# Moving transposes of x, wk, q and k from the PE to the DMA crossbar in a tuned attention and token-MLP kernel

## The chip, the cores and the metric

The kernel runs on one core of one Trainium2 chip. The metric is the device time of one execution in microseconds (us). In a ratio, the mean time of one kernel's fast runs is divided by the mean of the other's fast runs of the same rounds, so it is not quite the ratio of the medians quoted beside it. A run is called slow if it lies over 1.5% above the fastest of its kernel. A single run has no known state.

Names: PE is the matmul engine, PEld its weight loads, DVE the vector engine, ACT the scalar engine, POOL the GpSimd engine, SP or SyncE the engine that issues most DMAs. SBUF is the on-chip memory of the tiles, PSUM the one that PE's results go to. A DMA *lands* when its data have arrived.

## The reference, cut to what matters

```
def _attn_ref(q, k, v):                      # 8 batches, 12 heads, 448 positions, 64 wide
    scores = scale * np.matmul(q, k.transpose(0, 1, 3, 2)) - np.log(S)
    attn = 1.0 / (1.0 + np.exp(-scores))     # a sigmoid, no row sums
    return np.matmul(attn, v)
def _moe_ref(x, w_q, w_k, w_out):            # x: the heads side by side, 448 x 768
    wq, wk = x @ w_q, x @ w_k                # 768 -> 64
    W_tok = scale * np.einsum('bsd,btd->bst', wq, wk)
    mixed = np.einsum('bst,btd->bsd', W_tok, x)
    return np.maximum(mixed, 0.0) @ w_out
```

## The kernel before

Two batches and two heads form a pair. There are 24 pairs, in four units of six. A unit is two batches; its six pairs make the whole x of those batches, and then its MLP can run. The kernel's matmuls contract over the partitions, so q, k, x and wk are needed in a second, transposed layout. The kernel before makes all of these on the PE, with an identity matrix, into PSUM, and DVE copies the result out.

The order of work is written by hand. A string of letters says what is emitted next: S is one scores block and its sigmoid, P one block of values, q or k a transposition for a later pair, x the transposition of a finished piece of x, W a step of x times the weights, N the transposition of wk, U and M (or m) the mixing and its relu, O a block of the output.

```
def tr(n, nm, split=False):                        # letters q and k
    fb, ps = bank([P, NI, 2, NP], BF16, "pt" + nm)
    t16 = ld.pop((nm + "16", n))
    for i in range(NI):                            # seven 128x128 transposes
        nc.tensor.transpose(ps[:, i]..., t16[:, i]..., ident16)
    t = p_qk.tile([P, 2, NI, NP], BF16, tag=nm + "t", name=nm + "t")
    ...                                            # DVE copies ps to t
```

Inputs are float32. A load (448 KB, issued by SyncE) brings a pair's q, k or v; GpSimd casts it to bf16; the transposition reads the cast. The helper `pump` keeps both going. The cast of q or k needs one of two bf16 buffers, and a load needs a float32 buffer that an earlier cast has emptied:

```
def pump_loads():
    ...
            if n >= 3 and (nm, n - 3) not in cast:
                break
            load1(n, nm, nc.sync)                  # SyncE, in the order of emission
def pump():
    ...
            back = 3 if nm == "v" else 2           # v has three buffers, q and k two each
            if n >= back and (nm, n - back) not in used:
                break
            cast1(n, nm, nc.gpsimd)                # GpSimd, in the order of emission
        cast.add((nm, n))
        pump_loads()
...
        elif t in "qk":
            tr(c, t)
            used.add((t, c))
            pump()                                 # at once: next cast, next load
```

So right after each q or k transposition, the cast that reuses its buffer is emitted, and right after this the load that reuses the cast's float32 buffer. Loads, casts and stores stand in this order in their engines' queues.

## Time and profile before

| | before |
|---|---|
| median | 210.54 us (210.08 to 210.99, 2 runs) |
| span in the profile | 209.4 us |
| PE busy | 197.0 us, 94% |
| ACT busy | 170.8 us, of which the 168 sigmoids 155.4 |
| sigmoids | from 6.47 to 177.70 us |

A page row of slices shows, for 40 equal parts of the span, the busy share in tenths. A row of groups shows the source line, the engine, the operation with its tiles, the number of instructions, then busy us and the mean in ns, then the idle time before them and what ended it. The lines of the kernel before are in the prediction.

### The profile page before, as it was taken

The page shows a single profiled execution, that of the slowest core. Times are in us where ns is not written, and L with a number is a line of the kernel's source. Part 1 is how long each engine was busy: PE and PEld are TensorE (multiplying, and loading weights), DVE is VectorE, ACT ScalarE, POOL GpSimd, SP SyncE. Part 2 cuts the span into 40 slices and gives each one's busy share as a digit, 9 for nine tenths or more (in the row PEclk, how much of TensorE's full clock was granted, in tenths as well). Part 3 has the DMA queues.
Part 4 walks back from the last instruction along what each step waited for, and adds up shares of the span by engine and source line. Part 5 has one row for each costly group of instructions (what it writes and reads, how often), then busy time and mean ns, then how long its engine had stood idle before and what let it go on. Part 6 is the DMA issues. An engine that isn't in the chain of part 4 may idle for free.

```text
span 209.4 us, 6320 instructions
## 1 busy us (share of the span) xinstructions
PE 197.0 (94%) x2630; PEld 117.5 (56%) x2630; DVE 121.9 (58%) x208; ACT 170.8 (82%) x193; POOL 72.6 (35%) x85
## 2 busy tenths in 40 slices
PE   8498988889999999999999999999999999999991
PEld 7254544556546656656656565655565555655561
DVE  2135555755598746664889675645788654554321
ACT  3689999979999999999998989889898998055220
POOL 2477755577877842730022700251110000000000
PEclk9759999999999999999999999999999999999999
DMA  5999999999999999997065463355203252154785
GB/s 174 374 381 380 381 173 290 381 384 384 383 384 383 379 381 385 399 389 253 5 199 130 145 181 79 78 147 195 51 29 78 75 152 70 27 134 104 200 203 174
DMA packets 28684, 47.59 MB, mean 227 GB/s; under 512 B 5360, under 2 KB 24432, under 8 KB 28656
## 3 DMA queue, kind: packets, MB, share of 16 engines
q1 hardware_dynamic: 27616, 45.03, 67.1%
q10 hardware_dynamic: 1040, 2.16, 2.7%
q8 instruction: 20, 0.33, 0.7%
q14 instruction: 8, 0.07, 0.1%
HBM read 36.18 MB, written 11.01 MB: 225 GB/s over the span
## 4 chain that ended last, share of the span: by engine, by line
PE 75%; DMA 16%; POOL 2%; SPq 1%; ACT 1%; issue 1%; DVE 1%; DVEq 0%; ACTq 0%; POOLq 0%
PE po L283 27%; PE sc L154 15%; PE pv L173 13%; DMA v<-in_v_dram 9%; DMA k<-in_k_dram 8%; PE px L191 5%; PE pw L215 3%; PE ptq L131 3%; PE ptk L131 3%; PE pt L240 3%; PE pm L264 2%; ACT at L159 1%; POOL k L118 1%; POOL v L118 1%; SPq L107 1%; PE pk L227 1%
## 5 line engine op out<-in xcount | busy, mean ns | idle before, releaser
L159 ACT ACTIVATE at<-sc,bias_t 128x896 bf16<-128x896 f32 x168 | 155.4, 1020 | 12.6 <-PE sc L154 11.7
L283 PE MATMUL po<-wout,mx 128*128 128x384 bf16 (+1 forms) x342 | 60.6, 324 | 0.0
L154 PE MATMUL sc<-qt,kt 64*64 64x448 bf16 x672 | 57.7, 367 | 2.5 <-ACT at L159 1.8
L283 PEld LDWEIGHTS <-mx 128*128 128x128 bf16 x342 | 30.9, 98 | 24.3 <-issue 7.0
L173 PE MATMUL pv<-at,v 64*64 64x448 bf16 x672 | 41.8, 352 | 1.1 <-POOL v L118 1.1
L178 DVE CAST xt<-pv 128x896 bf16<-128x896 f32 x24 | 26.2, 1091 | 23.4 <-PE pv L173 23.4
L308 DVE COPY o<-po 128x384 f32<-128x384 f32 x45 | 25.1, 557 | 24.7 <-PE po L283 24.4
L154 PEld LDWEIGHTS <-kt 64*64 64x64 bf16 x672 | 21.9, 105 | 23.7 <-issue 12.6
L118 POOL CAST q<-q 128x896 bf16<-128x896 f32 x23 | 21.5, 933 | 33.3 <-issue 26.3
L118 POOL CAST v<-v 128x896 bf16<-128x896 f32 x24 | 22.3, 934 | 22.6 <-PE pv L173 18.0
L118 POOL CAST k<-k 128x896 bf16<-128x896 f32 x23 | 21.5, 933 | 19.4 <-PE ptk L131 15.7
L173 PEld LDWEIGHTS <-v 64*64 64x64 bf16 x672 | 20.5, 107 | 11.2 <-POOL v L118 1.4
L138 DVE COPY kt<-ptk 128x896 bf16<-128x896 bf16 x23 | 14.3, 620 | 10.3 <-PE ptk L131 10.2
L196 DVE COPY xn<-px 128x512 bf16<-128x512 bf16 x48 | 18.0, 417 | 2.9 <-PE px L191 2.9
L306 ACT COPY o<-po 128x384 f32<-128x384 f32 x10 | 4.8, 478 | 15.7 <-PE po L283 15.7
L256 DVE TENSOR_SCALAR mx<-pm 128x896 bf16<-128x896 f32 x15 | 16.3, 1088 | 1.8 <-PE pm L264 1.4
L138 DVE COPY qt<-ptq 128x896 bf16<-128x896 bf16 x23 | 14.1, 619 | 4.5 <-PE ptq L131 3.7
L131 PE MATMUL ptq<-ident,q 128*128 128x128 bf16 x161 | 13.7, 228 | 1.4 <-POOL q L118 1.4
L191 PE MATMUL px<-ident,xt 128*128 128x128 bf16 x192 | 14.7, 220 | 0.2 <-DVE o L308 0.2
L191 PEld LDWEIGHTS <-xt 128*128 128x128 bf16 x192 | 11.6, 98 | 4.6 <-issue 3.8
L131 PE MATMUL ptk<-ident,k 128*128 128x128 bf16 x161 | 13.3, 224 | 0.6 <-POOL k L118 0.6
L131 PEld LDWEIGHTS <-q 128*128 128x128 bf16 x161 | 9.9, 102 | 6.7 <-issue 3.7
(43 smaller groups left out, 93.8 us busy)
## 6 DMA issues: line engine op xcount, KB each, us to landing
q<-in_q_dram SPq DMA_DIRECT2D x24, 448.0 KB, 8.0
v<-in_v_dram SPq DMA_DIRECT2D x24, 448.0 KB, 7.5
k<-in_k_dram SPq DMA_DIRECT2D x23, 448.0 KB, 7.8
out_dram<-o SPq DMA_DIRECT2D x44, 192.0 KB, 3.0
w<-in_moe_w_out_dram SPq DMA_DIRECT2D x6, 384.0 KB, 5.8
out_dram<-o ACTq DMA_DIRECT2D x10, 192.0 KB, 3.2
wqk<-in_moe_w_q_dram SPq DMA_DIRECT2D x2, 192.0 KB, 9.4
wqk<-in_moe_w_k_dram SPq DMA_DIRECT2D x2, 192.0 KB, 8.5
```

The lines of the kernel that those rows point to most:

```text
L118: eng.tensor_copy(out=t16.rearrange("p i b d -> p b i d"), in_=ld.pop((nm, n)).rearrange("p b (i d) -> p b i d", i=NI),)
L131: nc.tensor.transpose(ps[:, i].rearrange("p h n -> p (h n)"), t16[:, i].rearrange("p b d -> p (b d)"), ident16,)
L138: nc.vector.tensor_copy(out=t[:, hs], in_=ps[:, :, hs, :].rearrange("p i h n -> p h i n"))
L154: nc.tensor.matmul(sc[HALF[h], b2, 0:S], qk["k", n][HALF[b2], h, i, :], qk["q", n][HALF[b2], h].rearrange("p i n -> p (i n)"), start=True, ...
L159: nc.scalar.activation(at, sc[:, :, 0:S], ACTF.Sigmoid, bias=bias_t, scale=attn_scale)
L173: nc.tensor.matmul(ps[HALF[b2], h, 0:S], ld["v16", n][HALF[h], i, b2, :], ats[n, i][HALF[h], b2, :], start=(i == 0), stop=(i == NI - 1),)
L178: nc.vector.tensor_copy(out=xts[j][:, :, 0:S], in_=ps[:, :, 0:S])
L191: nc.tensor.transpose(ps[:, m, h].rearrange("p b d -> p (b d)"), xts[j][:, h, m * P : (m + 1) * P], ident16,)
L196: nc.vector.tensor_copy(out=xns[u][:, :, b2, 2 * HD * j : 2 * HD * (j + 1)].rearrange("p m (h d) -> p m h d", h=2), in_=ps[:, :, :, b2, :],)
L256: nc.vector.tensor_scalar(dst, ps, moe_scale, 0.0, ALU.mult, ALU.max)
L283: nc.tensor.matmul(ps, mxs[u][c].rearrange("p b s -> p (b s)")[:, m * P : (m + 1) * P], wout16[:, c, w0:w1], start=(c == 0), stop=(c == NC ...
L308: nc.vector.tensor_copy(out=o[:, nb * NB : (nb + 1) * NB], in_=ps)
```

## The change

The intent is to relieve the PE: from pair 12 on, q and k go through the crossbar of the DMA engines, SBUF to SBUF (letters a and b, 24 transfers of 229 KB), and so do x (X, 12 of 262 KB) and wk (n, 2 of 262 KB) of the two middle units. The layouts change to what the crossbar gives, q and k get 14 buffers instead of 8 so as to be transposed early, the weight load is halved, the start is reordered, and the string of letters is planned anew with the output blocks moved to where the PE is freed.

```
-    p_qk = pool("qk", 8)
+    p_qk = pool("qk", 14)
...
+    def tr_dma(n, nm):
+        t16 = ld.pop((nm + "16", n))
+        t = p_qk.tile([P, NI, P], BF16, tag=nm + "t", name=nm + "t")
+        nc.sync.dma_start_transpose(out=t, in_=t16.rearrange("p i b d -> p (i b d)"))
+        qk[nm, n] = t
...
+    def tr_x_dma(n):
+        u, j = pairs[n]
+        nc.sync.dma_start_transpose(
+            out=xn_of(u, j).rearrange("p h m x -> p (h m) x"),
+            in_=xts[j].rearrange("p h s -> p (h s)"),
+        )
...
+        if dma:        # in mlp_wkn
+            nc.sync.dma_start_transpose(
+                out=wkn[u].rearrange("p b m x -> p (b m) x"), in_=wqk.rearrange("p b s -> p (b s)")
+            )
+            return
...
+    def cast_weights():
+        nc.gpsimd.tensor_copy(out=wqk16[HALF[0]], in_=wqk32)
+        nc.gpsimd.dma_start(out=wqk16[HALF[1]], in_=wqk16[HALF[0]])
...
-        "SPPPSkqSWWWSWWWWSWWWWSWSx",
-        "SNPSPPPPSPPSUSqSMUmSMq",
...
+        "SPPPPSkSkWSWWWSWWWWSWWWWSbx",
+        "SSPPPPNSPPPSUSaSMaSb",
+        "SSMUXSbSMSaSPPPSPPPPX",
+        "SamaSMSbmPPPPSPPPXSOSS",
...
-        elif t in "qk":
-            tr(c, t)
-            used.add((t, c))
+        elif kind in "qk":
+            (tr if t == kind else tr_dma)(c, kind)
+            used.add((kind, c))
             pump()
```

More of the change, by code (lines that the diff above doesn't have):

```diff
@@ L84 @@
     wqk16 = singles.tile([P, H, P], BF16, name="wqk16")
-    wqk32 = singles.tile([P, H, P], F32, name="wqk32")
+    wqk32 = singles.tile([NP, H, P], F32, name="wqk32")
     ident = singles.tile([P, P], F32)
@@ L125, with tr @@
     qk = {}
-    def tr(n, nm, split=False):
-        fb, ps = bank([P, NI, 2, NP], BF16, "pt" + nm)
+    def tr(n, nm):
+        fb, ps = bank([P, NI, P], BF16, "pt" + nm)
         t16 = ld.pop((nm + "16", n))
         for i in range(NI):
-            nc.tensor.transpose(
-                ps[:, i].rearrange("p h n -> p (h n)"),
-                t16[:, i].rearrange("p b d -> p (b d)"), ident16,
-            )
-        t = p_qk.tile([P, 2, NI, NP], BF16, tag=nm + "t", name=nm + "t")
-        def evac(hs):
-            nc.vector.tensor_copy(
-                out=t[:, hs], in_=ps[:, :, hs, :].rearrange("p i h n -> p h i n")
-            )
+            nc.tensor.transpose(ps[:, i], t16[:, i].rearrange("p b d -> p (b d)"), ident16)
+        t = p_qk.tile([P, NI, P], BF16, tag=nm + "t", name=nm + "t")
+        nc.vector.tensor_copy(out=t, in_=ps)
         qk[nm, n] = t
         free1.append(fb)
-        if split:
-            return evac
-        evac(slice(0, 2))
+    def tr_dma(n, nm):
+        t16 = ld.pop((nm + "16", n))
+        t = p_qk.tile([P, NI, P], BF16, tag=nm + "t", name=nm + "t")
+        nc.sync.dma_start_transpose(out=t, in_=t16.rearrange("p i b d -> p (i b d)"))
+        qk[nm, n] = t
     ats = {}
@@ L154, in scores @@
                 nc.tensor.matmul(
-                    sc[HALF[h], b2, 0:S], qk["k", n][HALF[b2], h, i, :],
-                    qk["q", n][HALF[b2], h].rearrange("p i n -> p (i n)"), start=True, stop=True,
+                    sc[HALF[h], b2, 0:S].rearrange("p (i n) -> p i n", i=NI),
+                    qk["k", n][HALF[b2], i, HALF[h]], qk["q", n][HALF[b2], :, HALF[h]],
+                    start=True, stop=True,
                 )
@@ L182, with xn_of @@
     xns = {}
+    def xn_of(u, j):
+        if j == 0:
+            xns[u] = p_x.tile([P, NJ, 2, 4, P], BF16, tag="xn", name="xn")
+        return xns[u][:, j]
     def tr_x(n):
         u, j = pairs[n]
-        if j == 0:
-            xns[u] = p_x.tile([P, 4, 2, D], BF16, tag="xn", name="xn")
-        fb, ps = bank([P, 4, 2, 2, HD], BF16, "px")
+        fb, ps = bank([P, 2, 4, P], BF16, "px")
         for h in range(2):
             for m in range(4):
-                nc.tensor.transpose(
-                    ps[:, m, h].rearrange("p b d -> p (b d)"), xts[j][:, h, m * P : (m + 1) * P],
-                    ident16,
-                )
-        for b2 in range(2):
-            nc.vector.tensor_copy(
-                out=xns[u][:, :, b2, 2 * HD * j : 2 * HD * (j + 1)].rearrange(
-                    "p m (h d) -> p m h d", h=2
-                ),
-                in_=ps[:, :, :, b2, :],
-            )
-        free1.append(fb)
+                nc.tensor.transpose(ps[:, h, m], xts[j][:, h, m * P : (m + 1) * P], ident16)
+        nc.vector.tensor_copy(out=xn_of(u, j), in_=ps)
+        free1.append(fb)
+    def tr_x_dma(n):
[4 more added lines that the diff above has]
+        )
     wkn, tmps, mxs = {}, {}, {}
@@ L215, in mlp_wqk @@
                 nc.tensor.matmul(
-                    ps[HALF[x], b2, 0:S], wqk16[HALF[b2], h, 64 * x : 64 * x + 64],
+                    ps[HALF[x ^ b2], b2, 0:S], wqk16[HALF[b2], h, 64 * x : 64 * x + 64],
                     xts[h // 2][HALF[b2], h % 2, 0:S], start=(h == 0), stop=(h == H - 1),
@@ L221, in mlp_wqk, with mlp_wkn @@
             free2.append(fb)
-    def mlp_wkn(u):
-        fb, ps = bank([P, 4, 2, P], BF16, "pk")
+    def mlp_wkn(u, dma=False):
+        wkn[u] = p_one.tile([P, 2, 4, P], BF16, tag="wkn", name="wkn")
+        if dma:
[3 more added lines that the diff above has]
+            return
+        fb, ps = bank([P, 2, 4, P], BF16, "pk")
         for b2 in range(2):
             for m in range(4):
-                nc.tensor.transpose(ps[:, m, b2, :], wqk[:, b2, m * P : (m + 1) * P], ident16)
-        wkn[u] = p_one.tile([P, 4, P], BF16, tag="wkn", name="wkn")
-        nc.vector.tensor_copy(
-            out=wkn[u], in_=ps.rearrange("p m b x -> p m (b x)")[:, :, 64:192]
-        )
+                nc.tensor.transpose(ps[:, b2, m], wqk[:, b2, m * P : (m + 1) * P], ident16)
+        nc.vector.tensor_copy(out=wkn[u], in_=ps)
         free1.append(fb)
@@ L240, in mlp_tmp @@
                 nc.tensor.matmul(
-                    ps[HALF[b2]], wkn[u][:, m, 64 * b2 : 64 * b2 + 64],
-                    xns[u][:, m, b2, nb * NB : (nb + 1) * NB],
+                    ps[HALF[b2]].rearrange("p (x d) -> p x d", d=HD), wkn[u][:, b2, m, HALF[1 - b2]],
+                    xns[u].rearrange("p j h m x -> p (j h) m x")[:, 6 * nb : 6 * nb + 6, m, HALF[b2]],
                     start=(m == 0), stop=(m == 3),
@@ L326, in load_weights @@
     def load_weights():
-        for b2 in range(2):
-            for x, w in enumerate((moe_w_q, moe_w_k)):
-                o = 64 * (x ^ b2)
-                nc.sync.dma_start(
-                    out=wqk32[HALF[b2], :, o : o + 64], in_=w.rearrange("(h d) n -> d h n", d=HD)
-                )
+        for x, w in enumerate((moe_w_q, moe_w_k)):
+            nc.sync.dma_start(
+                out=wqk32[:, :, 64 * x : 64 * x + 64], in_=w.rearrange("(h d) n -> d h n", d=HD)
+            )
+    def cast_weights():
+        nc.gpsimd.tensor_copy(out=wqk16[HALF[0]], in_=wqk32)
+        nc.gpsimd.dma_start(out=wqk16[HALF[1]], in_=wqk16[HALF[0]])
     def load_wout(c):
@@ L336, in load_wout @@
         nc.sync.dma_start(out=w32[c], in_=moe_w_out[c * P : (c + 1) * P, :])
+    PLAN = (
+        "SSSKSSSkqPPPPS",
+        "SPkSqSSPqSPqSkSPP",
+        "SPPPSxPSPSSPPSkSkP",
+        "SPPPPSSqSkSqqSPPPSx",
+        "SqPSSPPPSqSSxSxq",
+        "SPPPPSPPPSkSqSSxkPPSPk",
+        "SPPPPSkSkWSWWWSWWWWSWWWWSbx",
+        "SSPPPPNSPPPSUSaSMaSb",
+        "SSMUXSbSMSaSPPPSPPPPX",
+        "SamaSMSbmPPPPSPPPXSOSS",
+        "SbOaSPPPPSPPPXSOSSSO",
+        "SaSPPPSPPPPXSOSSSOO",
+        "SPPPSPPPPXSbSWWWWWSWWWWSWWWSa",
+        "SPPPSPPPPSnaSSSUUXSbO",
+        "SMSbSPPPPSPPPXSOSMSO",
+        "SMOSMSbOSMSOaSSMOPPPP",
+        "SPPPXSbSPPSPPPPPXSOSS",
+        "SbOSPPPPSPPPXSOSSSaO",
+        "SPPPPSPPPXSaSWWSWWWWWSWWWWWSO",
+        "SSSnOSPPPSPPPPSUUS",
+        "SMOOSSPPPPPPPSOSMSbOSM",
+        "SxOSPPPSPPPPSOSMSOxSM",
+        "SxOmPPSPPPPPSOSSSOOS",
+        "SOxSPPPSPPPPSOSSWWWWxS",
+        "WWWPPPPWPPPWWOxWWOONOUUMMMOOOmMmOOOOOOOOOOOOOOOO",
+    )
     IA, IB = slice(0, 4), slice(4, 7)
@@ L349, in cols @@
         return slice(r.start * HD, r.stop * HD)
-    nc.sync.dma_start(out=q0, in_=src["q"])
-    nc.sync.dma_start(out=k0[:, :, cols(KA)], in_=src["k"][:, :, cols(KA)])
-    nc.sync.dma_start(out=k0[:, :, cols(KB)], in_=src["k"][:, :, cols(KB)])
+    for t32, nm in ((q0, "q"), (k0, "k")):
+        for b2, eng in ((0, nc.sync), (1, nc.scalar)):
+            eng.dma_start(out=t32[:, b2], in_=src[nm][:, b2])
     nc.vector.memset(zeros, 0.0)
@@ L362, with keep_warm @@
     nc.scalar.activation(warm, bias_t, ACTF.Sigmoid, bias=bias_t, scale=1.0)
-    fb, ps = bank2("pwarm")
-    for _ in range(32):
-        nc.tensor.matmul(ps[:, 0, 0:P], zeros, zeros, start=True, stop=True)
-    free2.append(fb)
+    def keep_warm(n):
+        fb, ps = bank([P, 512], F32, "pwarm")
+        for _ in range(n):
+            nc.tensor.matmul(ps[:, 0:P], zeros, zeros, start=True, stop=True)
+        free1.append(fb)
+    keep_warm(32)
     for t in xts + [wqk]:
         nc.vector.memset(t[:, :, S:], 0.0)
-    ORDER = [("q", 1), ("k", 1), ("v", 0)]
-    nq = 2
-    for n in range(1, N):
-        for _ in range(2 if n in (1, 2, 3, 4) else 1):
-            if nq < N:
-                ORDER += [("q", nq), ("k", nq)]
-                nq += 1
-        ORDER.append(("v", n))
-    for n, at_ in ((0, 18), (1, 30), (2, 33), (3, 36), (4, 39), (5, 42), (6, 45)):
-        ORDER.insert(at_, ("w", n))
+    STEPS = "".join(PLAN)
+    ORDER, seen = [], dict(q=1, k=1, P=0)
+    first = {}
+    for t in STEPS:
+        t = dict(a="q", b="k").get(t, t)
+        if t in "qkP":
+            if t != "P":
+                ORDER.append((t, seen[t]))
+            elif seen[t] % NI == 0:
+                ORDER.append(("v", seen[t] // NI))
+            seen[t] += 1
+        first.setdefault(t, len(ORDER))
+    places = [(first["W"] - 9, 0)] + [(first["O"] - 14 + 2 * c, c) for c in range(1, 7)]
+    for n, (place, c) in enumerate(places):
+        ORDER.insert(place + n, ("w", c))
+    CASTS = list(ORDER)
+    n = CASTS.index(("w", 0))
+    CASTS.insert(n + 3, CASTS.pop(n))
     used, loaded, cast = set(), set(), set()
@@ L396, in pump @@
     def pump():
-        while len(cast) < len(ORDER) + 2:
-            nm, n = ORDER[len(cast) - 2]
+        while len(cast) < len(CASTS) + 2:
+            nm, n = CASTS[len(cast) - 2]
             if (nm, n) not in loaded:
@@ L405, in pump @@
                 else:
-                    nc.gpsimd.tensor_copy(out=wqk16, in_=wqk32)
+                    cast_weights()
             else:
@@ L425 @@
     for nm in "qk":
-        qk[nm, 0] = p_qk.tile([P, 2, NI, NP], BF16, tag=nm + "t", name=nm + "t")
+        qk[nm, 0] = p_qk.tile([P, NI, P], BF16, tag=nm + "t", name=nm + "t")
     def tr_part(nm, t16, r, e, b=None):
-        shape = [P, r.stop - r.start, 2, NP]
+        shape = [P, r.stop - r.start, P]
         fb, ps = (None, ps_q.tile(shape, BF16, tag=b, name="pt" + nm)) if b else bank(shape, BF16, "pt" + nm)
@@ L432, in tr_part @@
             nc.tensor.transpose(
-                ps[:, i - r.start].rearrange("p h n -> p (h n)"),
-                t16[:, i].rearrange("p b d -> p (b d)"), ident16,
+                ps[:, i - r.start], t16[:, i].rearrange("p b d -> p (b d)"), ident16,
             )
-        COPY[e](out=qk[nm, 0][:, :, r], in_=ps.rearrange("p i h n -> p h i n"))
+        COPY[e](out=qk[nm, 0][:, r], in_=ps)
         if fb:
@@ L441 @@
     tr_part("q", q016, IB, "s")
+    keep_warm(5)
     tr_part("k", k016, KA, "v", free2[-1])
+    keep_warm(3)
     used |= {("q", 0), ("k", 0)}
     pump()
-    PLAN = (
-        "SSSKqSSSSkq",
-        "SPPPPPSkSSPkSPqSS",
-        "SxPqSPPPPSPPSqSPPSkPSPP",
-        "SxPSSPkSSSkPPSkP",
-        "SPPPPSqSqSSqxSxSk",
-        "SSqkPPSPPPPSPqSkSSxPPPP",
-        "SPPPSkqSWWWSWWWWSWWWWSWSx",
-        "SNPSPPPPSPPSUSqSMUmSMq",
-        "SkSMxSkSPPPSPPPPSqSk",
-        "SMxmqSPPPPSPPPSOSSSOO",
-        "SSkxSSOkSPPPSPPPPSO",
-        "SSSqOkSPPPSPPPPSqxSPPPP",
-        "SPPPSOSSSqOxSWWWWWSWW",
-        "SWWWWWSOSSSNxPPPPPSPPSUU",
-        "SMSxkSPPPPSPPPSOSMSkO",
-        "SMmOkSMSOqSMSqOSPPPPSPPP",
-        "SOSSSkOxSPPPSPPPPSxO",
-        "SSSOOSSxOSPPSPPPPPPPPP",
-        "SPPPSxqSWSWWWWWWSWWWSWWOS",
-        "SSONSSOxSPPPPPPSPSUU",
-        "SSMxOSSPPPPPPPSOSMSkx",
-        "SPPPSPPPPmOSMmqOSMSOqSS",
-        "SkOxSPPPPSPPPSOSSSOOx",
-        "SPSPPPPPPSOSSSOOxS",
-        "WPPPWPPPPWWWWWWWWWWOONxOUUMmmOOmMmOOOOOOOOOOOOOOOO",
-    )
-    done = dict.fromkeys("SPqkKxWNUMO", 0)
+    done = dict.fromkeys("SPqkKxWNUMOD", 0)
     done["q"] = done["k"] = 1
-    for t in "".join(PLAN).replace(" ", ""):
-        kind = "M" if t == "m" else t
+    for t in STEPS:
+        kind = dict(m="M", a="q", b="k", X="x", n="N").get(t, t)
         c = done[kind]
@@ L492 @@
                 pump()
-        elif t in "qk":
-            tr(c, t)
-            used.add((t, c))
+        elif kind in "qk":
+            (tr if t == kind else tr_dma)(c, kind)
+            used.add((kind, c))
             pump()
+        elif t == "D":
+            fb, ps = bank([P, 512], F32, "pwarm")
+            for x in range(2):
+                nc.tensor.matmul(
+                    ps[HALF[x], 0:S].rearrange("p (i n) -> p i n", i=NI), zeros[HALF[0], 0:64], qk["q", 0][HALF[0], :, HALF[x]],
+                    start=True, stop=True,
+                )
+            free1.append(fb)
         elif t == "K":
@@ L500 @@
             tr_x(c)
+        elif t == "X":
+            tr_x_dma(c)
         elif t == "W":
             mlp_wqk(*divmod(c, H))
-        elif t == "N":
-            mlp_wkn(c)
+        elif kind == "N":
+            mlp_wkn(c, t == "n")
         elif t == "U":
```

## The prediction

> **What bounds the kernel now.** I read the page first: busy shares, then the slices.
>
> ```profile
> PE 197.0 (94%) x2630; PEld 117.5 (56%) x2630; DVE 121.9 (58%) x208; ACT 170.8 (82%) x193; POOL 72.6 (35%) x85
> ...
> PEclk9759999999999999999999999999999999999999
> DMA  5999999999999999997065463355203252154785
> ...
> L159 ACT ACTIVATE at<-sc,bias_t 128x896 bf16<-128x896 f32 x168 | 155.4, 1020 | 12.6 <-PE sc L154 11.7
> ```
>
> PE is busy almost all the time, but ACT is close behind, and a mean share hides that the two take turns. The clock is full except at the start. The DMA engines are full up to slice 18 (about 95 us) and a third to a half busy afterwards. The sigmoid row is the second limit: 168 sigmoids cost 155.4 us whatever PE does, and ACT waited only 12.6 us for PE before them. Next come busy times by stage:
>
> ```profile
> 60.00:100.00 40.00, 39.96 (x588) 24.40 (x590) 26.69 (x45) 38.91 (x44) 20.03 (x22) 1.00 0.99 363
> 100.00:140.00 40.00, 40.00 (x565) 23.50 (x558) 27.68 (x43) 35.93 (x39) 11.58 (x13) 1.00 0.43 118
> 140.00:177.00 37.00, 37.00 (x494) 21.80 (x496) 24.98 (x42) 33.78 (x38) 2.80 (x3) 1.00 0.34 94
> 177.00:209.40 32.40, 27.91 (x256) 16.60 (x248) 11.92 (x20) 9.70 (x17) 0.00 (x0) 1.00 0.55 144
> ```
>
> The columns are stretch, length, then PE, PEld, DVE, ACT, POOL busy, clock, DMA share, GB/s. From 60 us to 177 us PE is never idle, while ACT idles 1.1, 4.1 and 3.2 us. So the middle is PE-bound, by a narrow margin. After 177 us there are no sigmoids; this tail is PE alone. The ACT timeline shows the margin as small gaps before scores:
>
> ```profile
> 103.02 6.65 ACT L159 ACTIVATE at<-sc,bias_t 128x896 bf16<-128x896 f32 x7 [0.48 <-PE sc L154]
> 109.95 1.01 ACT L159 ACTIVATE at<-sc,bias_t 128x896 bf16<-128x896 f32 x1 [0.28 <-PE sc L154]
> ```
>
> It also gives three fixed points: the first sigmoid starts at 6.47, the last (176.69, 1.01 long) ends at 177.70, and 29 in a row take 26.25 us, so one costs 0.905 us. A PE timeline gives what PE pays for each kind of work, by start-to-start times (the second column includes pipeline drain):
>
> ```profile
> 160.51 0.55 PE L131 MATMUL ptq<-ident,q 128*128 128x128 bf16 x7
> 161.00 0.76 PE L154 MATMUL sc<-qt,kt 64*64 64x448 bf16 x12
> 161.69 0.56 PE L131 MATMUL ptk<-ident,k 128*128 128x128 bf16 x7
> 162.09 1.14 PE L283 MATMUL po<-wout,mx 128*128 128x384 bf16 x6
> 163.07 0.61 PE L191 MATMUL px<-ident,xt 128*128 128x128 bf16 x8
> 163.61 0.38 PE L154 MATMUL sc<-qt,kt 64*64 64x448 bf16 x4
> 163.82 0.93 PE L173 MATMUL pv<-at,v 64*64 64x448 bf16 x16
> ```
>
> Seven transposes of q or k cost 0.49 before 64-wide work (161.00 - 160.51) and 0.40 before full-array work; eight of x 0.54. A group of four scores or values costs about 0.19 to 0.23, a block of six output matmuls 0.98. Changing between 64*64 and 128*128 work costs about 0.1.
>
> **What the Trainium skill says.** "VectorE: DVE Perf Modes", section "The three transpose paths", gives 390 ns for a 128x128 transpose on TensorE and 1309 ns on the DMA crossbar. The trace has 220 to 228 ns per PE transpose and, pipelined, 0.40/7 = 57 ns; no DMA transpose has run yet. "DMA: Bandwidth & Descriptors", section "Latency and other measured facts", gives a DMA transpose 261 GB/s, or 350 to 400 when contiguous. The trace before has only plain transfers, but warns about small pieces: the wqk weight rows (256 B each) pull a full DMA from 380 down to about 130 GB/s, in this view of 20 to 30 us in 40 slices:
>
> ```profile
> GB/s 380 387 373 373 387 387 380 373 380 380 380 387 380 373 387 387 366 387 387 380 380 387 373 387 387 422 303 309 257 193 134 133 134 119 126 129 131 142 115 142
> ```
>
> The same page, section "Anatomy of one DMA — SWDGE (gpsimd) path", says that DMA engines do not wait on semaphores; the wait happens on the issuing sequencer before dispatch. The trace agrees: SyncE's queue itself waits, and everything behind waits too.
>
> ```profile
> SPq L318 <- DVE o L308: 48.4, 20, 7.2
> SPq L107 <- POOL k L118: 14.7, 8, 10.7
> ```
>
> **The change part by part.**
>
> *Removed from PE:* 24 q/k sets of 7 transposes, 12 x sets of 8, 2 wk sets of 8: 24 x 0.45 + 12 x 0.54 + 2 x 0.54 = 18.4 us, all on the bounding engine before 177 us. DVE loses their evacuations (24 x 0.62, 24 half copies of 0.42, two of wk), but it was not the limit.
>
> *Why not 18 us faster:* ACT takes over as bound. I added up each row of both plans (seven sigmoids a row) with the PE costs above and, for ACT, 0.905 per sigmoid and 0.8 per relu. Before, rows 9 to 23 sum to PE 107.3 against ACT 98.2; the trace takes 108.3 (68.4 to 176.7), so the bookkeeping holds. Summing the larger of PE and ACT over all 24 rows gives 165.2 before, against 171.2 measured (6.47 to 177.70): 3.4 of the remaining 6 us are start gaps (1.77, 0.16, 0.25, 1.25), 2.6 spread out. After, ACT alone sums to 154.4 (two relus fewer). PE is far below it in rows 7 to 14 and above it only in rows 15 and 20 to 23, by 1.3 + 1.4 + 1.1 + 0.7 + 0.5 = 5.1, because output blocks moved there. So 159.5, plus 1 us of start gaps and 2 spread out: 162.5.
>
> *Start:* the first k needs all 448 KB instead of 192, so the first sigmoid slips from 6.47 to about 7. In return three scores follow at once after the second k part, which should close the 1.77 gap; the two duplicate weight loads (256 B rows, issues of 2.74 and 3.75 us on SyncE) are replaced by an on-chip copy. Both are in the 1 us above.
>
> *Tail:* from 176.4, PE works until 205.1, 28.7 us. The new last row has 4 wqk steps fewer (-0.76), 2 output blocks more (+1.96): about 30.0.
>
> *Sum without new waits:* sigmoids end at 7 + 162.5 = 169.5; the tail starts 1.3 before, 168.2, and ends at 198.2; final stores 4.3 (205.1 to 209.4 now): 202.5 span; the unprofiled time is 1.1 above the span: 203.6 us.
>
> *Added:* 38 DMA transposes, 24 x 229 KB + 14 x 262 KB = 9.2 MB, all on SyncE's queue. At the 261 GB/s of the page that is 35 us of DMA (estimate), at the 130 of the 256 B pieces 70 us. They fall between about 55 and 140 us. Half of that has a full DMA now, but q and k transposes have a lead of 15 to 48 sigmoids (14 to 43 us) over their first use, thanks to 14 buffers instead of 8. The x ones lead by about 10 us, wk by about 6 us after its last matmul. I add 0.9 us for waits: **204.5 us**.
>
> **Rivals.**
>
> *ACT bounds earlier than hoped, or gains vanish in local bunching.* Rows 15 and 20 to 23 stay PE-bound and only three PSUM pairs buffer scores. Against: my sums already charge this. If the spread-out idle doubles: 206 to 207, "same".
>
> *SyncE's queue becomes the limit.* In the changed order a load often follows a transpose, and waits for a GpSimd cast that needs the buffer which that transpose reads. Thus one load holds up the queue for a transpose's whole latency plus 0.93 of cast. Ahead of the first wk transpose there is such a chain: x, k, load, load, load, q, wk. If a transpose takes 2 to 3 us, wk lands about when tmp needs it; at 6 us PE waits several us, twice, and stores back up behind. That makes 207 to 215.
>
> *The DMA rate becomes the limit.* Loads, stores and weights needed by 140 us are about 42 MB, 110 us at 380 GB/s. With 35 us of transposes this just fits; with 70 it lags by 40, more than the leads: 215 or more. For it: 256 B pieces at 130 GB/s. Against: those read HBM, these read SBUF.
>
> *The transposes are hidden but PE cools.* In rows 7 to 9 PE is only 55 to 70% busy; between 5 and 10 us a 46% busy PE lost its clock (0.81, then 0.50). Gaps here are under 1 us, so I hold it unlikely.
>
> **Range and chances.** With no waits and a better start, 201; with a few us of waiting for wk or x, 208 to 211. Range 200.5 to 211. Faster by over 2% means below 206.3: 0.62. Within 2%: 0.23. Slower, if queue or rate limits: 0.15.
>
> **What would show it.** Right: PE busy down by about 18 us to 179; ACT above 95% from 60 to 168 us; last sigmoid ending near 169.5; tail of 30 us; no long waits of PE weight loads for DMA transposes. Wrong: PE waiting for xn, wkn, kt or qt from DMA; SyncE waiting long for GpSimd casts; DMA at 9 in slices 18 to 27 with GB/s well below 380; PEclk below 9 in the middle; a transpose taking over 5 us from issue to landing.

## The result and the profile after

The changed kernel takes **295.4 us** (294.8 to 296.01, 2 runs) against 210.54: ratio 1.4031, 95% interval 1.3852 to 1.4211. Its outputs are correct. The prediction, 204.5 us and most likely faster, is wrong by 91 us.

From the page of the changed kernel: the busy row, the slices, and two groups.

```profile
PE 200.7 (68%) x2358; PEld 107.1 (36%) x2358; DVE 103.1 (35%) x149; ACT 168.7 (57%) x190; POOL 72.4 (25%) x86
...
PE   8788989850340846843800689968804999999993
...
ACT  3999999980060348560830188859900688941421
...
PEclk9999999975555689795865599979975899999998
DMA  7999989996667758789297536949998234404686
...
L156 ACT ACTIVATE at<-sc,bias_t 128x896 bf16<-128x896 f32 x168 | 156.1, 1021 | 96.3 <-PE sc L150 95.6
```

Up to slice 8 (59 us) PE and ACT are about as busy as in the kernel of before. From then on PE and ACT both stop and start again, and the granted clock falls to half in the stops. ACT now waits 95.6 us for scores, where it waited 11.7. The DMA engines are not the obvious limit: there are slices with 2 to 5 tenths among them. What holds up the PE shows in the list of waits (engine, line, what it waits for; us in total, times, longest), all engines of the changed kernel:

```profile
POOL k L118 <- DMA kt<-k: 48.1, 6, 15.4
POOL q L118 <- DMA qt<-q: 41.6, 5, 11.4
...
PE pv L170 <- POOL v L118: 35.8, 6, 14.2
...
PE pt L241 <- DMA wkn<-wqk: 29.5, 2, 17.3
```

PE hardly waits for a transposed q or k, which I had looked at, with its lead of 14 to 43 us. It waits for the **cast of v**, which no part of the change touches (35.8 us), and for wk, in two stops (29.5 us). The transposes of wk are late before they begin: they are issued at 158.97 and 221.40 us and land 5.4 and 3.2 us later, but by the time of the issue PE has stood for 11.8 and 8.9 us. GpSimd in its turn waits 89.7 us for crossbar transposes to leave the bf16 buffers. The timelines of 57 to 80 us show how these hang together. SyncE's queue of the changed kernel (start, us, engine, line, transfer):

```profile
57.60 2.39 SPq L140 DMA_TRANSPOSE kt<-k  x1
67.52 0.36 SPq L339 DMA_DIRECT2D w<-in_moe_w_out_dram  x1
67.93 0.43 SPq L107 DMA_DIRECT2D k<-in_k_dram  x1
68.41 0.46 SPq L107 DMA_DIRECT2D v<-in_v_dram  x1
68.91 0.47 SPq L107 DMA_DIRECT2D k<-in_k_dram  x1
69.42 1.40 SPq L140 DMA_TRANSPOSE qt<-q  x1
77.50 0.37 SPq L107 DMA_DIRECT2D q<-in_q_dram  x1
77.91 0.47 SPq L107 DMA_DIRECT2D v<-in_v_dram  x1
```

GpSimd of the changed kernel, same stretch (in brackets the idle time before it, and what ended it):

```profile
65.79 0.93 POOL L118 CAST k<-k 128x896 bf16<-128x896 f32 x1 [8.17 <-DMA kt<-k]
66.67 0.83 POOL L452 CAST wout<-w 128x768 bf16<-128x768 f32 x1
76.54 0.93 POOL L118 CAST q<-q 128x896 bf16<-128x896 f32 x1 [9.04 <-DMA qt<-q]
77.41 0.93 POOL L118 CAST v<-v 128x896 bf16<-128x896 f32 x1
```

Follow it once. At 57.60 SyncE issues a transposition of k. The next cast of k needs the buffer that it reads, so it starts only at 65.79, 8 us later. The cast of wout stands behind it on GpSimd and ends at 67.50. The load that needs the buffer of that cast is the next entry of SyncE's queue, so SyncE stands from 60.0 to 67.5. Only then come the loads behind it, and the next transposition at 69.42. Then it goes round again: 76.54, 77.50. The cast of v at 77.41 stands behind the cast of q, and PE needs that v. ACT's timeline shows the price:

```profile
61.82 3.70 ACT L156 ACTIVATE at<-sc,bias_t 128x896 bf16<-128x896 f32 x4 [0.55 <-PE sc L150]
80.22 1.01 ACT L156 ACTIVATE at<-sc,bias_t 128x896 bf16<-128x896 f32 x1 [14.70 <-PE sc L150]
```

The DMA view of the same 57 to 80 us in 40 slices says that the engines stand still in ten of the slices while PE waits, so their rate alone does not hold up this stretch. In most of the others they are full, so the landings of 7 to 8 us contain their rate too:

```profile
DMA  9999999999982800000097999899999370000938
```

I call this **the loop**: transposition, cast into its buffer, load into that cast's buffer, next transposition. The 24 q and k transposes are issued from 57.6 to 233.5 us, one per 7.6 us on the mean (175.9/23), while their own issue takes 1.2 to 3.3 us.

### The profile page after: what moved, and what is told of

The parts are those of the page before. It is cut to its first block, busy times and chain, and to the rows that moved or that the text cites. A ratio compares the mean times of both kernels' runs of the same rounds, so it can differ in the third digit from the quotient of the medians.

```text
span 294.2 us, 5749 instructions
## 1 busy us (share of the span) xinstructions
PE 200.7 (68%) x2358; PEld 107.1 (36%) x2358; DVE 103.1 (35%) x149; ACT 168.7 (57%) x190; POOL 72.4 (25%) x86
## 4 chain that ended last, share of the span: by engine, by line
PE 29%; DMA 11%; issue 8%; SPq 8%; ACT 2%; DVE 2%; POOL 2%; DVEq 0%; ACTq 0%; POOLq 0%
PE po L284 15%; PE sc L150 4%; PE pv L170 4%; DMA out_dram<-o 3%; DMA kt<-k 3%; SPq L140 3%; DMA wkn<-wqk 3%; PE pt L241 2%; SPq L197 2%; ACT at L156 2%; DMA qt<-q 2%; PE pw L213 2%; SPq L319 2%; SPq L107 1%; DVE xt L175 1%
## 5 line engine op out<-in xcount | busy, mean ns | idle before, releaser
L156 ACT ACTIVATE at<-sc,bias_t 128x896 bf16<-128x896 f32 x168 | 156.1, 1021 | 96.3 <-PE sc L150 95.6
L170 PE MATMUL pv<-at,v 64*64 64x448 bf16 x672 | 48.2, 396 | 37.1 <-POOL v L118 35.8
L150 PE MATMUL sc<-qt,kt 64*64 64x448 bf16 x672 | 62.4, 384 | 9.9 <-ACT at L156 7.3
L241 PE MATMUL pt<-xn,wkn 128*64 128x384 bf16 x64 | 9.3, 448 | 29.5 <-DMA wkn<-wqk 29.5
L257 DVE TENSOR_SCALAR mx<-pm 128x896 bf16<-128x896 f32 x19 | 20.5, 1090 | 5.5 <-PE pm L265 5.5
L213 PE MATMUL pw<-xt,wqk 64*64 64x448 bf16 x192 | 13.8, 398 | 9.1 <-DVE xt L175 9.1
L241 PEld LDWEIGHTS <-wkn 128*64 128x64 bf16 x64 | 4.3, 142 | 33.2 <-DMA wkn<-wqk 30.1
L213 PEld LDWEIGHTS <-wqk 64*64 64x64 bf16 x192 | 7.0, 121 | 13.0 <-issue 9.6
L192 DVE COPY xn<-px 128x1024 bf16<-128x1024 bf16 x12 | 8.3, 688 | 5.8 <-PE px L191 5.8
L265 PE MATMUL pm<-wqk,tmp 64*64 64x448 bf16 x96 | 9.2, 401 | 0.7 <-ACT at L156 0.6
L133 DVE COPY kt<-ptk 128x896 bf16<-128x896 bf16 x11 | 6.8, 620 | 7.6 <-PE ptk L131 7.6
```

The source lines that it names most:

```text
L150: nc.tensor.matmul(sc[HALF[h], b2, 0:S].rearrange("p (i n) -> p i n", i=NI), qk["k", n][HALF[b2], i, HALF[h]], qk["q", n][HALF[b2], :, HAL ...
L156: nc.scalar.activation(at, sc[:, :, 0:S], ACTF.Sigmoid, bias=bias_t, scale=attn_scale)
L170: nc.tensor.matmul(ps[HALF[b2], h, 0:S], ld["v16", n][HALF[h], i, b2, :], ats[n, i][HALF[h], b2, :], start=(i == 0), stop=(i == NI - 1),)
L213: nc.tensor.matmul(ps[HALF[x ^ b2], b2, 0:S], wqk16[HALF[b2], h, 64 * x : 64 * x + 64], xts[h // 2][HALF[b2], h % 2, 0:S], start=(h == 0), ...
L241: nc.tensor.matmul(ps[HALF[b2]].rearrange("p (x d) -> p x d", d=HD), wkn[u][:, b2, m, HALF[1 - b2]], xns[u].rearrange("p j h m x -> p (j h ...
L257: nc.vector.tensor_scalar(dst, ps, moe_scale, 0.0, ALU.mult, ALU.max)
```

## The experiments

The theory is the loop. The rivals: the crossbar's **rate** (too many bytes in small pieces), the **new plan** itself (a bad order even without DMA transposes), and the **rest of the change** (layouts, start, weights). All kernels of one group ran on one chip, beside runs of the kernel before of 209.7 to 210.7 us median (one run, 212.2 us, beside the kernel that costs the transposition). All but the four marked "wrong" gave correct outputs. "One run" means that the state is unknown.

### Which part: all on PE, four buffers, each part alone

Every a, b, X and n of the plan goes back to q, k, x and N; nothing else changes:

```
-        "SSMUXSbSMSaSPPPSPPPPX",
+        "SSMUxSkSMSqSPPPSPPPPx",
```

> The changed kernel with every crossbar transpose put back on the PE (new plan, layouts, buffers and start kept). Both theories, that of the loop through the shared in-order queues and that of a slow crossbar, say the loss comes from the DMA transposes alone: 206 to 213 us. If the new plan or the new tile layouts are at fault, over 230 us.

Measured: 228.39 us, ratio 1.0845 (1.0785 to 1.0905). Without the DMA transposes 67 of the 295 us are gone, so most of the loss is theirs. But the new plan on the PE costs 18 us more than the old, which I had not expected. In its waits of the PE stands `px<-xt` with 12.0 us in 10 times: in the new plan x follows right behind the values whose copy by DVE it needs. With x by the crossbar (the second of the two runs of parts below) PE does not have this wait.

Two more bf16 buffers for each of q and k:

```
-    p_c16 = pool("c16", 2)
+    p_c16 = pool("c16", 4)
-                back = 3 if nm == "v" else 2
+                back = 3 if nm == "v" else 4
```

(and 12 instead of 14 buffers of q and k, for room).

> Four buffers instead of two for the cast q and k, casts running up to four ahead (12 instead of 14 buffers for the transposed tiles, for space). Theory 'loop': a cast waits for the transpose that reads its buffer, the v cast and the next load wait behind that cast, and the next transpose waits behind that load; with two more buffers the loop opens and the time falls below 240 us, GpSimd's waits for kt and qt from 90 us to under 20. Rival 'crossbar rate': 38 transposes at some 4.5 us each are the limit whatever the buffers, time stays over 280 us.

Measured: 260.01 us, ratio 1.2358 (1.2284 to 1.2432). It helps by 35 us, not by the most of it, and neither expectation came. GpSimd still waits 45.7 us for transposes (90 before) and PE 22.1 for v. With more buffers `pump` runs ahead as far as they allow, and then again the next cast is the one that needs the buffer just given to the crossbar.

The changed kernel with only q and k by DMA, and with only x and wk:

> Only q and k from pair 12 on by DMA; x and wk on the PE. Theory 'loop': most of the loss stays, 260 to 290 us. If the loss comes from PE's waits for wk and x, it falls below 230 us.

> Only x and wk of the two middle units by DMA; q and k on the PE. Theory 'loop': no cast waits for a transpose, so 205 to 218 us, with PE waits of a few us for wk. Rival 'crossbar rate': 14 of 38 transposes, so some 14/38 of the 85 us, 235 to 245 us.

Measured, one run each: 265.71 and 222.81 us. With q and k alone PE waits 26.4 us for v and 19.2 for xt. With x and wk alone it waits 6.5 for xt and 2.7 for wk, and the time lies between the two expectations. The q and k transposes, whose buffers feed casts, carry most of it. But the parts do not add up: against the all-PE run (228.39) q and k alone cost 37 us and x and wk alone gain 6, while all together cost 67. PE's wait for wk points to a reason: 2.7 us here, 29.5 where the transposes of q and k stand in the same queue.

### The cost of a crossbar transposition by itself

A kernel of its own: twelve transposes of 128x896 bf16 in a row, a chain of dependent ones, twelve plain copies of the same size, and three times a transposition behind four 448 KB loads. Its output is wrong, which doesn't matter for the time.

```
for t in ta: nc.sync.dma_start_transpose(out=t, in_=src)          # ta: twelve in a row
for t in tb: nc.sync.dma_start_transpose(out=t, in_=prev); prev = t # tb: each needs the last
for t in tcs: nc.sync.dma_start(out=t, in_=cs)                    # tc: plain copies
# td: four loads ahead of each
```

> Wrong result on purpose: it measures the disputed cost by itself. A: twelve 128x896 crossbar transposes back to back on an otherwise empty queue; B: a chain of four, each waiting for the one before; C: twelve plain copies of the same 229 KB; D: three times four loads of 448 KB and then a transpose. Theory 'loop': alone a transpose lands in 2.5 to 4 us and the queue passes one per 1.3 to 1.6 us (150 to 180 GB/s), behind four loads it takes 6 to 8 us. Rival 'crossbar rate': even alone the queue passes one per 4 us or more.

From SyncE's timeline of this kernel, and below that from its list of DMA issues (KB each where the page has it, median us from issue to landing):

```profile
1.35 16.08 SPq L32 DMA_TRANSPOSE ta<-src  x12
...
32.20 7.69 SPq L50 DMA_DIRECT2D tc<-cs  x12
```

```profile
tc<-cs SPq DMA_DIRECT2D x12, 224.0 KB, 2.3
ta<-src SPq DMA_TRANSPOSE x12, 3.1
tb<-tb SPq DMA_TRANSPOSE x3, 2.9
td<-ds SPq DMA_TRANSPOSE x3, 7.4
```

A transposition costs SyncE 1.34 us to issue (16.08/12), a plain copy 0.64. In a row, transposes land 1.33 us apart, which is 172 GB/s (229 KB/1.33); copies land 0.65 apart, 351 GB/s. From 6 to 17 us of this run SyncE issues transposes without a break and the DMA engines are 90 to 93% busy, so the run does not tell which of the two sets the 172. Alone a transposition lands after 2.9 us, but behind four loads after 7.4. In the changed kernel those of q and k land after 4.5 us in the median (3.0 to 8.1). So neither the issue nor the rate of the crossbar by itself fills 7.6 us per transposition; that the rest is the wait behind loads and casts is read from the timelines above.

### Opening the loop

The cast and load that need a transposed buffer are emitted 24 letters after the transposition, when it should have landed (four bf16 buffers and 12 of q and k, as in the run of four buffers; the deferral ends early where a later step needs the cast):

```
-            (tr if t == kind else tr_dma)(c, kind)
-            used.add((kind, c))
-            pump()
+            tr_dma(c, kind)
+            later.append((step + 24, (kind, c)))   # used.add and pump() happen then
```

> Same 38 transposes as the changed kernel and four cast buffers, but after each q or k transpose the casts and loads that need its freed buffer are put into the queues only 24 plan steps later (some 7 us), when the transpose has landed. Theory 'loop': GpSimd no longer waits for kt or qt (under 10 us in all instead of 90), v is cast in time, and the time falls below 230 us, well below the 260 of four buffers alone. Rival 'crossbar and DMA load': the transposes take DMA time (1.31 us each alone) that the loads lack, whatever the order: 250 us or more.

Measured: 245.94 us, ratio 1.1674 (1.161 to 1.1739). Order and buffers together, with the same transposes, take 49 us off the 295; over four buffers alone (260.01) the new order takes 14. Both expectations were missed, and it is not the end. Of the PE's waits 14.8 us for wk, 9.8 for v and 6.8 for xt are left, and GpSimd still waits 35.7 for transposes. Between 64 and 124 us SyncE now issues almost without a break, and its issues stretch; from its timeline:

```profile
64.95 3.71 SPq L140 DMA_TRANSPOSE kt<-k  x1
68.77 5.59 SPq L140 DMA_TRANSPOSE qt<-q  x2
```

All on the PE again, with x four letters later than in the first experiment:

> All transposes on the PE again, but the twelve x ones 4 plan steps after the place of the DMA ones, so that PE does not wait for the eviction of xt in front of them (12.0 us of such waits in the first such run). If those waits are what made the new plan slow on the PE: 211 to 218 us. If the new plan or layouts cost more: still over 222.

Measured: 215.61 us, ratio 1.0239 (1.0161 to 1.0317). Of the 18 us that the new plan cost on the PE, 13 were the place of x; 5 remain.

The deferred version with only q and k by DMA, x (four letters later) and wk on PE; and the deferral with two bf16 buffers:

> As the deferred run, but only q and k by DMA; x (4 steps later) and wk on the PE. Theory 'loop': with the loop open q and k by DMA cost nothing: 205 to 220 us, against 266 undeferred. Rival 'DMA load': over 245.

> Deferral alone, with the two cast buffers and 14 tile buffers of the changed kernel; the deferral ends early wherever the next transpose needs its cast. Theory 'loop': between the changed kernel (295) and the deferred run with four buffers, 240 to 275 us.

Measured: 228.14 us, ratio of the fast runs (224.67 and 227.78) 1.074 (1.0621 to 1.0859), its profiled run slow; and 251.91 us (one run). The first misses both its expectations: with q and k alone by DMA and deferred it still lies about 11 us above the all-PE run with x later. Deferral alone does nearly what both do, 252 against 246, while four buffers alone gave 260. So the order in the queues alone takes 43 of the 49 us, and the buffers alone take 35: either one opens most of the loop, the order somewhat more.

### The rest of the change, and hybrids with the old plan

The old plan in the changed kernel, all on PE:

> The changed kernel's code (tile layouts, start, weight copy, 14 buffers) with the plan of the kernel before and every transpose on the PE. If layouts, start and weight copy are neutral, 207 to 213 us, same as before; if they are what cost the 5 us that the new plan shows on the PE, 214 to 218.

Measured: 211.38 us, ratio 1.0054 (0.9984 to 1.0124). Layouts, start and halved weights are neutral to within about 1%, which removes that rival.

The old plan with q and k of pairs 14 to 21 (16 transposes), or of pairs 16 to 21 (12), by DMA, with the deferral and four buffers:

> The plan of the kernel before in the changed kernel's code; only q and k of pairs 14 to 21 by DMA (16 transposes), four cast buffers, dependents deferred by 24 plan steps; x, wk and the last two pairs on the PE. Theory 'loop': with the loop open and the DMA less full, PE loses 16 x 0.45 = 7 us in the stretch where it is the bound: 203 to 208 us. Rival 'crossbar costs in any case': 212 or more.

> As the one before, from pair 16 on (12 transposes), so that the first comes when the DMA is less full. Theory 'loop': 12 x 0.45 = 5 us less: 204 to 209 us, and no wait of GpSimd for a transpose over 3 us. Rival: 212 or more.

Measured: 210.72 us, ratio 1.0006 (0.9965 to 1.0047); and 212.97 us, ratio 1.013 (1.0073 to 1.0188), the latter with one gap of 3.08 us at 43 us behind a v cast. Both miss what the loop theory expected. In the first the transposes are hidden: no stall of PE for one is left. Sixteen sets have left the PE, 16 x 0.45 = 7.2 us by my count, and the time has not moved. ACT waits 11.6 us for scores, as before (11.7), and between 60 and 140 us the PE is busy 77.20 us of 80 where it was busy 79.96. So a part of what was taken off the PE has become idle time of the PE.

### Transposes that cost nothing

The changed kernel without any DMA transpose; consumers read the last tile that the PE transposed. Wrong, and free of races. This is the ceiling of the new plan.

```
     def tr_dma(n, nm):
-        t16 = ld.pop((nm + "16", n))
-        ...
-        nc.sync.dma_start_transpose(...)
+        ld.pop((nm + "16", n))
+        qk[nm, n] = qk[nm, 11]
```

> Wrong result on purpose: the changed kernel with its DMA transposes left out and nothing in their place (consumers read the last tile that the PE transposed), all else kept. It measures the sum without new waits of the prediction: 203.6 us if that sum holds (201 to 206). If local bunching of PE work between the scores keeps ACT idle, as in the run from pair 14 on where 7 us less PE work changed nothing, 207 to 212.

Measured: 210.84 us (208.66 to 212.72), ratio 0.9964 (0.9905 to 1.0024). **Even free transposes bring no gain clear of noise with this plan.** So the 84.6 us above it (295.4 - 210.84) are waits that the transfers cause; by the waits of ACT for scores it is 95.6 - 11.8 = 83.8. And the gain that I had forecast was missing as well.

A part of where it went shows between 66 and 77 us, in the rows with few blocks for the PE. ACT and PE of the ceiling, each in its timeline:

```profile
71.42 1.01 ACT L154 ACTIVATE at<-sc,bias_t 128x896 bf16<-128x896 f32 x1 [2.05 <-PE sc L148]
72.91 1.01 ACT L154 ACTIVATE at<-sc,bias_t 128x896 bf16<-128x896 f32 x1 [0.49 <-PE sc L148]
```

```profile
69.22 1.71 PE L168 MATMUL pv<-at,v 64*64 64x448 bf16 x16 [0.93 <-POOL v L118]
...
72.73 2.05 PE L279 MATMUL po<-wout,mx 128*128 128x384 bf16 x6
...
75.40 1.15 PE L279 MATMUL po<-wout,mx 128*128 128x384 bf16 x6
```

The same block of six output matmuls takes 2.05 us and then 1.15. The slices of the granted clock show 5 and 8 there, and 9 elsewhere but for the last (8). PE was 63% busy from 60 to 70 us, with gaps of less than 1 us, and its granted clock was 0.50 from 68 to 74 us. ACT idled 2.05 + 0.49 + 1.29 = 3.8 us around it, at the time that it should have been the bound. Not all of this is the clock: in the first of the three gaps PE also waited 0.93 us for a cast of v.

### Bytes against order

Transposes of about half the bytes (the rest of each tile is set to zero by DVE; wrong), once in the changed kernel, once in the deferred one:

```
-        nc.sync.dma_start_transpose(out=t, in_=t16...)
+        nc.sync.dma_start_transpose(out=t[:, 0:3], in_=t16[:, 0:3]...)
+        nc.vector.memset(t[:, 3:7], 0.0)
```

> Wrong result on purpose: the changed kernel with 38 transposes of about half the bytes (3 of 7 or 4 of 8 blocks; the other blocks filled by VectorE), same order and waits. Theory 'loop of latencies': each turn of the loop loses only the transfer part, some 0.7 of 7.3 us: 270 to 288 us. Rival 'rate': the excess of 85 us over the kernel before is roughly halved, 245 to 260.

> Wrong result on purpose: the deferred run (246 us) with half the bytes per transpose. If what is left there is DMA and queue time of the transposes (DMA share 1.0 from 65 to 125 us, issues stretched to 2 to 5 us), it falls to 218 to 232. If it is the order of the queue alone, over 238.

Measured: 275.32 us in the fast run (a slow one of 280.6), and 233.91 us, ratio 1.1122 (1.1085 to 1.1159). Half the bytes take 20 of 295 us off the changed kernel: the loop stays, with landings of 4.0 to 4.1 us (4.5 with all bytes) and 82.9 us of GpSimd's waiting for transposes. In the deferred version they take 12 of the 35 us that it lies above the ceiling.

All transposes issued from ACT's queue instead of SyncE's:

```
-        nc.sync.dma_start_transpose(...)
+        nc.scalar.dma_start_transpose(...)
```

> The changed kernel with all 38 transposes issued from ScalarE's queue instead of SyncE's (still one transposing stream). A transpose then no longer stands behind a load that waits for a cast, nor a load behind a transpose; ACT pays 38 issues of 1.2 us and more. Theory 'loop through SyncE': 225 to 260 us, GpSimd's waits for kt and qt under 40 us. If SyncE's queue has no part in it: still 285 or more.

Measured: 271.88 us, ratio 1.2928 (1.2878 to 1.2978): better by 23 us, but far less than expected. The waits of ACT in this run begin:

```profile
ACT at L156 <- issue: 31.5, 10, 5.0
ACT at L156 <- PE sc L150: 25.1, 26, 6.7
```

The sigmoids now wait in the same in-order queue as the transposes, which wait for casts and copies. Waiting for v has gone from the PE's list; GpSimd still waits 81.3 us for transposes. The queue was changed, but the casts and the buffers that a transposition holds were not. What SyncE's part of the loop is worth by itself this run does not tell, since ACT's queue now stalls in its place.

### What is left in the deferred version, and one more candidate

The deferred version with the two transposes of wk back on PE (n to N in the plan):

> The deferred version (246 us) with one more thing undone: the two transposes of wk go back to PE; q, k and x stay on the crossbar. If PE's wait for wk in the deferred version (14.8 us in its list of waits) is time of its own on the path, this run takes 231 to 235. If wk only waits because everything behind the full queue is late, PE stops a little later for the v cast or for x instead, and the run stays at 240 to 246.

Measured: 236.44 us, ratio 1.1261 (1.1217 to 1.1305), between the two expectations. Of the 14.8 us that PE waited for wk, about 9 were wk's own (9.5 by the medians, 8.7 by the ratios); the rest has turned into a wait of 4.7 us for a transposition of x, which was not in the list before.

The candidate: the new plan with x later, x and wk on PE, deferral, and q and k of pairs 14 to 21 alone by DMA:

> A candidate: the changed schedule with x four steps later and x and wk on PE (all on PE that took 215.6), with q and k of pairs 14 to 21 alone by the crossbar (16 transposes) and the casts deferred. 16 sets of 0.45 us off PE are 7 us: if they count, 208 to 210, below the kernel before; if the gains vanish between ACT and PE as in the other hybrid, 212 to 216; if the first transposes still stall the v cast as when pairs 12 to 23 were moved, 220 to 228.

Measured: 223.57 us, ratio 1.059 (1.0529 to 1.0651), the third expectation. No correct version tried is faster than the kernel before. The hybrid with 16 transposes and the old plan equals it.

| version | us | ratio to before |
|---|---|---|
| changed kernel | 295.4 | 1.403 |
| four bf16 buffers | 260.0 | 1.236 |
| deferral, two buffers (one run) | 251.9 | |
| deferral, four buffers | 245.9 | 1.167 |
| the same, wk on PE | 236.4 | 1.126 |
| deferral, four buffers, half the bytes (wrong) | 233.9 | 1.112 |
| new plan all on PE, x later | 215.6 | 1.024 |
| old plan, 16 transposes, deferral | 210.7 | 1.001 |
| new plan, free transposes (wrong) | 210.8 | 0.996 |

## Why the prediction was wrong

**The step that failed most** is "I add 0.9 us for waits". In its place the runs show some 84 us. I had argued that q and k transposes "have a lead of 15 to 48 sigmoids (14 to 43 us) over their first use". That guards the reader of the result. It does not guard the next user of the buffer that is read, nor whatever stands behind that user in a queue. Here these are the casts on GpSimd, v among them, and the loads on SyncE.

**The second rival named this mechanism** ("one load holds up the queue for a transpose's whole latency plus 0.93 of cast"), and its signs came true: "SyncE waiting long for GpSimd casts" (64.6 us at the loads of q, k and v, 34.7 before), and "PE waiting for xn, wkn" (29.5 us for wkn). The size was wrong, 207 to 215 us. I counted it ahead of the two transposes of wk, instead of at each of the 24 transposes of q and k. The landing that I took, 2 to 6 us, held in the median (4.5 us; 8 in the first turn of the loop): the count failed, not the landing. Nor did I follow GpSimd's queue on to the cast of v. That the order is the cause of the larger part is shown by deferral (295 to 252 in one run, buffers unchanged) and supported by the half-size transposes, which leave the loop nearly as it was.

**The rate** as a rival was half right. In the changed kernel it is not the bound by itself: the engines stand still within the loop, though half the bytes win 20 us there too. Once the loop is open, the DMA row of slices reads 9 up to 122 us, and half the bytes win 12 us. The rate measured alone was 172 GB/s, between the 130 and the 261 I used. Of the 35 us that the deferred version keeps above the ceiling, 12 go with the bytes and about 9 with wk; the two have not been shown to add, and the rest stays open. That it is the order of the full queue is only argued.

**The gain was mis-sized too.** The forecast without waits was 203.6; the ceiling ran at 210.8. Its trace tells where, from its first sigmoid at 7.46 to the end of the last at 175.97:

| term | forecast | ceiling |
|---|---|---|
| first sigmoid | 7 | 7.46 |
| ACT's work in the sigmoid phase | 154.4 | 157.9 |
| idle of ACT in the rows bound by the PE | 5.1 | 5.8 |
| idle at the start, and the rest of it | 1 | 1.0 |
| "spread out" | 2 | in the row of ACT's work |
| the three gaps of ACT around the half clock | 0 | 3.8 |
| last sigmoid to the PE's end | 28.7 | 29.0 |

A sigmoid with its neighbours costs about 0.92 us, not the 0.905 of the one tight run of 29 that I took, and before too it was 155.4/168 = 0.925. "PE cools" I had held unlikely because the gaps are under 1 us; it happened, once. And there was little to win: ACT idled only 12.0 us in the whole sigmoid phase of the kernel before (171.23 less 159.28 busy), and 11.5 are left with free transposes (168.51 less 156.99; the table has the 10.6 that its timeline lists as gaps). The old plan with 16 hidden transposes says the same: what the PE loses there does not reach ACT. This is the first rival, bunching, and it alone would have made "same" the likely answer even without the loop. Two slips of the prediction are small: its five rows sum to 5.0 and not 5.1, and of the 12.6 us that it reads as ACT's waiting for PE, 11.7 were for PE.

**What held.** 280 transposes less on the PE, with 8 more warm-up matmuls, make 2630 - 2358 = 272 instructions less. But PE's busy time is 187.5 in the ceiling and not 179, partly for the half clock. The first gap after the start, 1.77 us, is closed: the ceiling has 39 sigmoids in a row from 7.46. The tail is 29 us, as reckoned.

The half clock in the changed kernel (0.84 on the mean) came with the stops. I take it for a consequence, but no run separates it. PE was busy 13 us longer there than with free transposes (200.7 against 187.5, the same 2358 instructions), which is an estimate of the most that it can have cost.

## What to carry to other kernels

In this kernel a transposition by DMA holds its source until it lands (3.0 to 8.1 us for q and k), and one on the PE holds it for half a microsecond (0.49): before moving one, follow each in-order queue from the buffer it reads, to the next writer of it, to all that stands behind this writer, and put those instructions later in program order, or give the source more buffers; here the order was worth 43 us alone (one run), two more buffers 35, both 49. Before moving work off the busiest engine, run the kernel with that work left out: here that experiment shows no gain to be had with this plan. If a plan was tuned around two engines that take turns, idle time of the second one is all that relief of the first can win while they take turns, and it is read in the trace of before: 12 us here, hard to reach.

## What the Trainium skill lacked or had wrong

- "Advanced Engine Details and Errata", section "X-Bar Transpose (TRN2)", says that transposing DMAs are as fast as regular ones, at 350 to 400 GB/s, and "DMA: Bandwidth & Descriptors", section "Latency and other measured facts", gives 261 GB/s or 350 to 400 when contiguous. From SBUF to SBUF, 128x896 bf16, nothing else running, twelve in a row on SyncE's queue, the run shows 172 GB/s, half of the 351 of a plain copy of the same size. Whether the issue on SyncE or the crossbar sets it, the run does not tell.
- No page read for this gives the time from issue to landing of such a transposition: 2.9 us alone, 3.1 in a row, 7.4 behind four loads of 448 KB. "VectorE: DVE Perf Modes", section "The three transpose paths", has one duration, 1309 ns for a 128x128 block; in the run, tiles of seven such blocks landed 1.33 us apart. Nor has any page, in microseconds, its issue on SyncE: 1.34 us against 0.64 for a plain copy, up to 3.71 in the deferred kernel, where SyncE issues almost without a break.
- No page read for this warns that the casts and loads that reuse the source of a DMA transpose close a loop through two in-order queues: 89.7 us of GpSimd's waiting, and 295.4 us against 251.9 (one run) with the same buffers and the casts emitted later.
- "TensorE: Matmul & The Clock Gate", section "Why this matters for your kernels", asks for no PE idle gaps over about 3 us. By itself that row is not enough: in the version with free transposes the granted clock was 0.50 from 68 to 74 us after gaps of less than 1 us, at 63% busy, and a block of six matmuls took 2.05 us instead of 1.15. The case is not new to the page: its section "A second HAM failure mode: psum-queue depth-cycling" tells of a clock that swings between half and full under frequent short idles of PE. The row of rules leaves it out.
